# Two MLP products done with seven half-size block products in place of eight, their weight operands streamed from scratch memory

## The chip, the cores and the metric

The kernel runs on one core of a Trainium2 chip. The metric is the device time in microseconds (us) of one execution; a time quoted for a kernel is the median of its runs. All runs of one set ran on one chip, beside runs of the kernel before. A ratio is the mean time of one kernel's fast runs over the mean of the other's in the same rounds, so it is not quite the ratio of the two medians that stand beside it; 95% intervals are in square brackets.

Terms: TensorE does the matrix products; VectorE, ScalarE and GpSimd do the element-wise work. SBUF is the memory that the kernel keeps its operands in, PSUM the one that TensorE's results go to; a bank is in this text one buffer of a PSUM pool, and so one tile of the pool `ps_f`. The bank guard is a name for waits in the compiled program that the trace of the changed kernel shows: a product that goes to one half of a tile waits for the engine that reads the other half (192 waits, 115.8 us; in e_banks, with a tile for each sum, none). A pass is one matmul record of the trace; each fp32 matmul of the kernel leaves two (1152 records for the 576 matmuls of the up product before). The granted clock is the share of TensorE's full clock that the profile recorded.

## The reference, shortened to what matters

```python
# q, k, v: (8, 8, 576, 64) fp32; attention inside chunks of 64 tokens, then x: (8, 576, 512)
def _moe_ref(x, w_ch1, w_ch2):                 # w_ch1: 512 x 2048, w_ch2: 2048 x 512
    X = np.fft.fft(np.fft.fft(x, axis=1), axis=2)
    u = x + np.real(X).astype(np.float32)
    un = (u - mean(u)) / np.sqrt(var(u) + 1e-06)          # over the last axis
    ch = np.maximum(un @ w_ch1, 0.0) @ w_ch2              # the two MLP products
    return (u + ch).astype(np.float32)
```

The weights arrive in double precision; the kernel rounds them to fp32 itself.

## The kernel before

The 4608 token rows are worked through in nine groups of 512. In each group TensorE does the up product (16 outputs of 128 x 512, four matmuls each) and the down product (four outputs, 16 matmuls each). The attention and Fourier work of the next batch is slipped in between: `mlp` is a generator, and at each `yield` some of that side work is issued. From the eighth group on there is none left; I call the eighth and the ninth the quiet groups. Before the first group, and beside it, the weights are rounded.

```python
ps_t = ctx.enter_context(tc.tile_pool(name="ps_t", bufs=2, space=bass.MemoryType.PSUM))
ps_a = ctx.enter_context(tc.tile_pool(name="ps_a", bufs=2, space=bass.MemoryType.PSUM))
ps_f = ctx.enter_context(tc.tile_pool(name="ps_f", bufs=2, space=bass.MemoryType.PSUM))
...
def round_weight(i):                          # cut: one 128 x 512 piece of the weights
    ...
    nc.vector.tensor_scalar(wi, hi, 0x000FFFFF, None, ALU.bitwise_and)
    nc.vector.tensor_scalar(p, hi, 0x7FF00000, None, ALU.bitwise_and)
    # cut: three ScalarE steps; then for the piece before:
    nc.vector.scalar_tensor_tensor(w, lo, 2.0 ** -52, w, ALU.mult, ALU.add)
    nc.vector.scalar_tensor_tensor(p, hi, 0x80000000, p, ALU.bitwise_and, ALU.bitwise_or)
    nc.gpsimd.tensor_tensor(out=w, in0=w, in1=p.bitcast(FP32), op=ALU.mult)
...
def mlp(g):
    unT = unTs.pop(g)
    h1 = one_p.tile([128, KF, G * 128], FP32, tag="big", name="h1")
    for m in range(KF):                                        # up product, KF = 16
        up = ps_f.tile([128, G * 128], FP32, tag="ff", name="up")
        for kk in range(KD):                                   # KD = 4
            nc.tensor.matmul(out=up[:, 0:cols], lhsT=w1[:, kk, m * 128:(m + 1) * 128],
                             rhs=unT[:, kk, 0:cols], start=(kk == 0), stop=(kk == KD - 1))
        nc.scalar.activation(out=h1[:, m, 0:cols], in_=up[:, 0:cols], func=ACTF.Relu)
        yield
    for s, n in enumerate(groups[g]):                          # down product
        dn = ps_f.tile([128, 512], FP32, tag="ff", name="dn")
        for m in range(KF):
            nc.tensor.matmul(out=dn, lhsT=h1[:, m, s * 128:(s + 1) * 128], rhs=w2[:, m, :],
                             start=(m == 0), stop=(m == KF - 1))
            # cut: transposes of the next group, yields
        nc.vector.tensor_tensor(out=o, in0=dn, in1=natural(n), op=ALU.add)
        store(n, o)
        yield
```

Of the kernel before, what the change touches and what calls it, by code (L numbers as in the profile page):

```python
# [8 lines left out]
FP32 = mybir.dt.float32  # L9
# [7 lines left out]
def kernel(  # L17
# [52 lines left out]
    three_p = ctx.enter_context(tc.tile_pool(name="three", bufs=3))  # L70
    sm_p = ctx.enter_context(tc.tile_pool(name="sm", bufs=4))
    ps_t = ctx.enter_context(tc.tile_pool(name="ps_t", bufs=2, space=bass.MemoryType.PSUM))
    ps_a = ctx.enter_context(tc.tile_pool(name="ps_a", bufs=2, space=bass.MemoryType.PSUM))
    ps_f = ctx.enter_context(tc.tile_pool(name="ps_f", bufs=2, space=bass.MemoryType.PSUM))

    ident = const.tile([128, 128], FP32, name="ident")
    sign = const.tile([128, 1], FP32, name="sign")
# [4 lines left out]
    cd = const.tile([128, 2, HM + 1], FP32, name="cd")  # L82
    cs = const.tile([128, DM], FP32, name="cs")
    sd = const.tile([128, HM - 1], FP32, name="sd")
    w1 = const.tile([128, KD, DFF], FP32, name="w1")
    w2 = const.tile([128, KF, DM], FP32, name="w2")


    LO, HI, RE = "lo", "hi", "rest"
# [26 lines left out]
    def xt(n):  # L116
        return xall[:, place[n], 0:DM + 1]
# [16 lines left out]
    def load(n):  # L134
        for src, dst, nm, eng in ((q, qs, "q", nc.sync), (k, ks, "k", nc.scalar if n == 0 else nc.sync)):
            if n < first[1]:
                i = 2 * n + (nm == "k")
                t = start[:, (4 + i) * DM:(5 + i) * DM].rearrange("p (h d) -> p h d", h=H)
            else:
                t = two_p.tile([128, H, D], FP32, tag=nm, name=nm)  # L140
            (b0, c0), (b1, c1) = chunks(n)
            if b0 == b1 and c1 == c0 + 1:
                parts = [(0, 128, b0, c0)]
            else:
                parts = [(0, CH, b0, c0), (CH, CH, b1, c1)]
            for p0, np_, b, c in parts:
                eng.dma_start(  # L147
                    out=t[p0:p0 + np_], in_=src[b, :, c * CH:c * CH + np_, :].rearrange("h p d -> p h d")
                )
            dst[n] = t  # L150
# [98 lines left out]
    def att_T(n):  # L249

        a = qs.pop(n)
        pt = turn(lambda j: a[:, 2 * j:2 * j + 2, :].rearrange("p h d -> p (h d)"))
        t = one_p.tile([128, 2 * NJ, CH + 1], FP32, tag="qT", name="qT")
        low = kind(n) == LO
        nc.scalar.copy(t[:, :, CH:0:-1] if low else t[:, :, 0:CH], pt.rearrange("p j (c t) -> p (j c) t", c=2))  # L255
        if low:
            nc.gpsimd.tensor_copy(t[:, :, 0:1], t[:, :, CH:CH + 1])  # L257
        qT[n] = t
        a2 = ks.pop(n)
        pt = turn(lambda j: a2[:, 2 * j:2 * j + 2, :].rearrange("p h d -> p (h d)"))  # L260
        t = one_p.tile([128, NJ, 128], FP32, tag="kT", name="kT")
        nc.vector.tensor_copy(t, pt)  # L262
        kT[n] = t

    def att_S(n):
        a, b = qT.pop(n), kT.pop(n)
# [63 lines left out]
    def shift(b):  # L330

        lows = [xt(at[LO, b, i]) for i in range(NM)]
        r = b % 2 * CH
        rest = xt(rests[b // 2])[r:r + 1, 0:DM]
        t = three_p.tile([128, XW], FP32, tag="y", name="first")
        for i in range(NM):
            nc.sync.dma_start(out=t[2 * i:2 * i + 2, 0:DM], in_=lows[i][0:CH + 1:CH, 0:DM])
        nc.sync.dma_start(out=t[2 * NM:2 * NM + 1, 0:DM], in_=rest)
        for i in range(NM):
            nc.sync.dma_start(out=lows[i][0:CH + 1:CH, 0:DM], in_=t[2 * i + 1:2 * i + 3, 0:DM])  # L340
        nc.sync.dma_start(out=rest, in_=t[0:1, 0:DM])

    def fold(b, i):

# [27 lines left out]
    def attention(b):  # L372

        lo, hi = first[b], first[b + 1] - 1

        def ready(n):
            if n == at[LO, b, NM - 1]:
                shift(b)
            for i in range(NM):
                if n == at[HI, b, i]:  # L380
                    fold(b, i)
            if n == at[HI, b, 0]:
                fold(b, NM)

        if b == 0:
            att_T(0)
        for n in range(lo, hi + 1):
            att_S(n)
            yield
            if n + 1 < NT:  # L390
                att_T(n + 1)
                if n + 3 < NT and n + 3 >= first[1]:
                    load(n + 3)
            yield
            if n > lo:
                att_V(n - 1)
                if n + 2 < NT:
                    load_v(n + 2)
                ready(n - 1)
                yield  # L400
            att_P(n)
            yield
        att_V(hi)
        if hi + 3 < NT:
            load_v(hi + 3)
        ready(hi)
        yield
# [97 lines left out]
    def turned(g, s):  # L505
# [8 lines left out]
        else:  # L514
            nc.scalar.copy(unT[:, :, s * 128:(s + 1) * 128], pt)  # L515

    def store(n, o):

        if kind(n) == LO:
            b, c = chunks(n)[0]  # L520
            to = out[b, c * CH + 1:c * CH + 129, :].rearrange("(c p) d -> c p d", c=2)
            nc.sync.dma_start(out=to[:, ::-1], in_=o)
            return
        for h, (b, c) in enumerate(chunks(n)):
            r0, t0 = h * CH, c * CH
            if kind(n) == RE:
                nc.sync.dma_start(out=out[b, t0 + 1:t0 + CH, :], in_=o[r0 + 1:r0 + CH])
                nc.sync.dma_start(out=out[b, 0:1, :], in_=o[r0:r0 + 1])
            else:
                nc.sync.dma_start(out=out[b, t0:t0 + CH, :], in_=o[r0:r0 + CH])  # L530

    PARTS = 4
    N_MLP = KF + G * PARTS
    N_READY = KF + 2 * PARTS

    def mlp(g):

        unT = unTs.pop(g)
        cols = 128 * len(groups[g])
        h1 = one_p.tile([128, KF, G * 128], FP32, tag="big", name="h1")  # L540
        for m in range(KF):
            up = ps_f.tile([128, G * 128], FP32, tag="ff", name="up")
            for kk in range(KD):
                nc.tensor.matmul(  # L544
                    out=up[:, 0:cols],
                    lhsT=w1[:, kk, m * 128:(m + 1) * 128],
                    rhs=unT[:, kk, 0:cols],
                    start=(kk == 0),
                    stop=(kk == KD - 1),
                )  # L550
            nc.scalar.activation(out=h1[:, m, 0:cols], in_=up[:, 0:cols], func=ACTF.Relu)  # L551
            yield
        for s, n in enumerate(groups[g]):
            dn = ps_f.tile([128, 512], FP32, tag="ff", name="dn")
            for m in range(KF):
                nc.tensor.matmul(  # L556
                    out=dn,
                    lhsT=h1[:, m, s * 128:(s + 1) * 128],
                    rhs=w2[:, m, :],
                    start=(m == 0),  # L560
                    stop=(m == KF - 1),
                )
                if m % (KF // PARTS) == KF // PARTS - 1:
                    i = s * PARTS + m // (KF // PARTS)
                    if g + 1 < NG:
                        for j in range(G):
                            due = G * PARTS - (2 * (G - j) if g > 0 else G - j + 1)
                            if i == due - 1:
                                normed(g + 1, j)
                            if i == due:  # L570
                                turned(g + 1, j)
                    if m < KF - 1:
                        yield
            o = three_p.tile([128, DM], FP32, tag="o", name="o")
            nc.vector.tensor_tensor(out=o, in0=dn, in1=natural(n), op=ALU.add)  # L575
            store(n, o)
            yield

    with tc.manual_schedule():
        make_identity(nc, ident)  # L580
# [26 lines left out]
        def round_next():  # L607
            nonlocal n_w
            if n_w <= len(pieces):
                round_weight(n_w)  # L610
                n_w += 1
# [25 lines left out]
        for b in range(1, B):  # L637
            n_tiles = first[b + 1] - first[b]
            sizes.append(4 * n_tiles + 4 + NM + b % 2)
        done, cur = 0, 0  # L640
        t = 0
        for g in range(NG):
            for _ in mlp(g):
                t += 1
                round_next()
                if t % 2:
                    round_next()
                if cur < len(sides):
                    t0 = KF + 1 if cur == 0 else N_READY + (cur - 1) * N_MLP + (2 if cur == 1 else 0)
                    t1 = N_READY + cur * N_MLP + (2 if cur == 0 else 0)  # L650
                    due = min(sizes[cur], (t - t0) * sizes[cur] // (t1 - t0 - 1))
                    while done < due:
                        next(sides[cur], None)
                        done += 1
                    if t >= t1 - 1:
                        for _ in sides[cur]:
                            pass
                        cur, done = cur + 1, 0
# [49 lines left out]
```

## Time and profile before

| | before |
|---|---|
| time, median of its first 3 runs | 1326.65 us (1326.09 to 1328.92) |
| profiled span, granted TensorE clock | 1325.4 us, 0.987 |
| TensorE busy | 1278.1 us, 96% |
| moved by DMA | 57.01 MB, 43 GB/s |
| first product starts / second group starts | 87.23 / 258.47 us |
| groups 2 to 7, mean of one | 140.0 us |
| eighth group | 111.6 us |

How to read it: the starts come from the TensorE timeline (the first row of the up product's line in each group), and a group's time is the difference of two of them; groups 2 to 7 are (1098.37 - 258.47) / 6. The first row of the second group, before:

```profile
258.47 3.60 PE L544 MATMUL up<-unT,w 128*128 128x512 f32 x8
```

A group is 110 us of MLP and, up to the seventh, some 30 us of attention and Fourier work on the same engine.

### The profile page before, as it was taken

What the parts mean: (1) busy time and instruction counts of PE and PEld (TensorE: products, weight loads), DVE (VectorE), ACT (ScalarE), POOL (GpSimd) and SP (SyncE); (2) the same over time, 40 slices, a digit from 0 to 9 for tenths busy, and PEclk for the clock granted to TensorE, in tenths of its full rate; (3) what the DMA queues carried; (4) which work ended last, traced back from release to release, by engine and by line L of the source; (5) the groups of instructions that cost most, each with busy time, mean ns of one, the idle gap of its engine ahead of it and who ended that gap; (6) DMA issues with size and microseconds to landing.
All of it is one profiled execution on the core that took longest, in us unless ns stands there. A gap on an engine that the chain in (4) does not pass through costs nothing.

```text
span 1325.4 us, 13849 instructions
## 1 busy us (share of the span) xinstructions
PE 1278.1 (96%) x5708; PEld 624.4 (47%) x5708; DVE 347.9 (26%) x648; ACT 253.6 (19%) x517; POOL 129.9 (10%) x188
## 2 busy tenths in 40 slices
PE   7788889999999999999999999999999999999998
PEld 5453344544444445444544445444444444444443
DVE  4479942421231114220321033211311130000000
ACT  3257620121011201121112111210111001100100
POOL 0135411002000201002100110020002010000000
PEclk9899988999999999999999999999999999999999
DMA  8634530221012101211022002210100000000000
GB/s 197 157 96 150 158 79 19 51 45 40 10 37 52 32 8 30 59 32 29 21 48 47 10 17 56 43 39 8 33 17 0 9 17 8 0 16 16 0 8 24
DMA packets 126261, 57.01 MB, mean 43 GB/s; under 512 B 116533, under 2 KB 117046, under 8 KB 126198
## 3 DMA queue, kind: packets, MB, share of 16 engines
q1 hardware_dynamic: 124598, 55.73, 17.1%
q8 instruction: 45, 0.74, 0.2%
q10 hardware_dynamic: 1600, 0.39, 0.2%
q14 instruction: 18, 0.15, 0.0%
HBM read 46.50 MB, written 9.44 MB: 42 GB/s over the span
## 4 chain that ended last, share of the span: by engine, by line
PE 85%; DVE 5%; DMA 3%; issue 2%; SPq 2%; ACT 1%; POOL 1%; POOLq 0%; DVEq 0%
PE dn L556 36%; PE up L544 34%; PE pt L245 4%; PE z L421 4%; PE mix L464 3%; DVE power L226 1%; PE xp L310 1%; DMA xall<-in_moe_w_ch_dram 1%; PE sc L272 1%; DVE power L234 1%; DVE w L224 1%; PE z L431 1%; SPq L157 1%; DVE w L233 1%; SPq L147 1%
## 5 line engine op out<-in xcount | busy, mean ns | idle before, releaser
L544 PE MATMUL up<-unT,w 128*128 128x512 f32 x1152 | 515.5, 598 | 8.6 <-ACT h L551 7.7
L556 PE MATMUL dn<-w,h 128*128 128x512 f32 x1152 | 518.5, 599 | 0.0
L544 PEld LDWEIGHTS up<-unT,w 128*128 128x128 f32 x1152 | 212.7, 190 | 253.7 <-issue 237.1
L556 PEld LDWEIGHTS dn<-w,h 128*128 128x128 f32 x1152 | 214.0, 191 | 246.6 <-issue 244.7
L551 ACT ACTIVATE h<-up 128x512 f32<-128x512 f32 x144 | 85.7, 595 | 423.9 <-PE up L544 423.8
L575 DVE TENSOR_TENSOR o<-dn,xall 128x512 f32<-128x512 f32 x36 | 24.8, 690 | 250.4 <-PE dn L556 250.4
L281 DVE TENSOR_REDUCE mx<-sc 128x8 f32<-128x512 f32 x36 | 24.9, 691 | 208.0 <-PE sc L272 208.0
L319 DVE TENSOR_TENSOR xall<-xp,rd 128x512 f32<-128x512 f32 x36 | 24.9, 690 | 131.2 <-PE xp L310 131.2
L479 POOL TENSOR_TENSOR xall<-y,xall 128x513 f32<-128x513 f32 x16 | 27.6, 1724 | 262.8 <-DVE y L472 262.8
L235 POOL TENSOR_TENSOR w<-w,power 128x512 f32<-128x512 f32 x32 | 44.6, 1395 | 65.9 <-DVE power L234 65.9
L421 PE MATMUL z<-tk,pm 128*128 128x289 f32 x128 | 37.9, 417 | 4.0 <-POOL pm L365 4.0
L439 ACT COPY zf<-z 128x256 f32<-128x256 f32 x32 | 11.9, 371 | 151.2 <-PE z L421 109.4
L289 ACT ACTIVATE ex<-ex 128x512 f32<-128x512 f32 x36 | 22.7, 629 | 94.1 <-DVE ex L283 94.1
L262 DVE COPY kT<-pt 128x512 f32<-128x512 f32 x36 | 24.5, 681 | 51.8 <-PE pt L245 51.8
L310 PEld LDWEIGHTS xp<-v,pT 64*64 64x64 f32 x1152 | 20.8, 138 | 30.0 <-issue 21.8
L421 PEld LDWEIGHTS z<-tk,pm 128*128 128x128 f32 x128 | 23.9, 192 | 22.1 <-issue 13.7
L257 POOL COPY qT<-qT 128x8 f32<-128x8 f32 x16 | 3.2, 201 | 314.1 <-ACT qT L255 314.1
L272 PEld LDWEIGHTS sc<-kT,qT 64*64 64x64 f32 x1152 | 21.3, 141 | 23.4 <-issue 23.4
L515 ACT COPY unT<-pt 128x512 f32<-128x512 f32 x18 | 10.5, 585 | 111.6 <-PE pt L245 111.6
L310 PE MATMUL xp<-v,pT 64*64 64x64 f32 x1152 | 25.8, 229 | 5.8 <-ACT pT L300 5.8
L291 DVE TENSOR_REDUCE rd<-ex 128x8 f32<-128x512 f32 x36 | 24.7, 686 | 25.0 <-ACT ex L289 25.0
L605 PE MATMUL idle<-warm 128*128 128x289 f32 x92 | 30.2, 466 | 0.0
(90 smaller groups left out, 791.8 us busy)
## 6 DMA issues: line engine op xcount, KB each, us to landing
xall<-in_moe_w_ch_dram SPq DMA_DIRECT2D x32, 512.0 KB
v<-in_v_dram SPq DMA_DIRECT2D x142, 64.0 KB
q<-in_q_dram SPq DMA_DIRECT2D x34, 128.0 KB
k<-in_k_dram SPq DMA_DIRECT2D x34, 128.0 KB
out_dram<-o SPq DMA_DIRECT2D x16, 256.0 KB
out_dram<-o SPq DMA_DIRECT2D x32, 128.0 KB
q<-in_q_dram SPq DMA_DIRECT2D x14, 256.0 KB
k<-in_k_dram SPq DMA_DIRECT2D x14, 256.0 KB
```

What stands on the lines that cost most here:

```text
L235: nc.gpsimd.tensor_tensor(out=w, in0=w, in1=p.bitcast(FP32), op=ALU.mult)
L245: nc.tensor.transpose(pt[:, j, :], src(j), ident)
L272: nc.tensor.matmul(out=sc[t0:t0 + CH, e, j * CH:(j + 1) * CH], lhsT=a[r0:r0 + D, 2 * j + c, 0:CH], rhs=b[r0:r0 + D, j, t0:t0 + CH], start= ...
L281: nc.vector.tensor_reduce(out=mx, in_=s4, axis=AX.X, op=ALU.max)
L310: nc.tensor.matmul(out=xp[t0:t0 + CH, e, j * D:(j + 1) * D], lhsT=a[r0:r0 + CH, j, t0:t0 + CH], rhs=b[r0:r0 + CH, c, j, :], start=True, st ...
L421: nc.tensor.matmul(out=z[:, 0:NQ], lhsT=pm[p, fold_, half], rhs=tk[p, i, fold_, :], start=(i == 0), stop=(i == NM), skip_group_check=(T == 2),
L464: nc.tensor.matmul(out=o[:, cols], lhsT=zt[:, T], rhs=tab, start=(T == 0), stop=(T == 3), skip_group_check=True,)
L479: eng.tensor_tensor(out=x[:, 0:w], in0=y[:, 0:w], in1=x[:, 0:w], op=ALU.add)
L544: nc.tensor.matmul(out=up[:, 0:cols], lhsT=w1[:, kk, m * 128:(m + 1) * 128], rhs=unT[:, kk, 0:cols], start=(kk == 0), stop=(kk == KD - 1),)
L551: nc.scalar.activation(out=h1[:, m, 0:cols], in_=up[:, 0:cols], func=ACTF.Relu)
L556: nc.tensor.matmul(out=dn, lhsT=h1[:, m, s * 128:(s + 1) * 128], rhs=w2[:, m, :], start=(m == 0), stop=(m == KF - 1),)
L605: nc.tensor.matmul(out=idle[:, 0:NQ], lhsT=warm[:, 0:128], rhs=warm[:, 0:NQ], start=True, stop=True)
```

## The change

Its intent: write each product as a 2 x 2 product of blocks and do it with seven products of half-size blocks for eight, as in the Strassen-Winograd scheme. TensorE then does 448 passes of 256 columns per group for 256 of 512 columns, an eighth less work. The price: the seven weight operands (some are sums of blocks) take 7/4 of the weights' room and are not kept on chip; they are formed once, beside the first group, stored to scratch memory, and streamed back in slabs by each later group; and the partial results are put together by VectorE, ScalarE and GpSimd. The first group still does eight products. The core of the diff:

```diff
-    ps_a = ctx.enter_context(tc.tile_pool(name="ps_a", bufs=2, space=bass.MemoryType.PSUM))
-    ps_f = ctx.enter_context(tc.tile_pool(name="ps_f", bufs=2, space=bass.MemoryType.PSUM))
+    ps_a = ctx.enter_context(tc.tile_pool(name="ps_a", bufs=1, space=bass.MemoryType.PSUM))
+    ps_f = ctx.enter_context(tc.tile_pool(name="ps_f", bufs=4, space=bass.MemoryType.PSUM))
+    dram = ctx.enter_context(tc.tile_pool(name="dram", bufs=1, space=bass.MemoryType.DRAM))
...
-                t = two_p.tile([128, H, D], FP32, tag=nm, name=nm)
+                t = one_p.tile([128, H, D], FP32, tag=nm, name=nm)
...
+    def keep1(f, kk):                    # four GpSimd sums and seven stores; keep2 is like it
+        ...
+            nc.gpsimd.tensor_tensor(out=out_, in0=in0, in1=in1, op=op)
+        to = s1.rearrange("m p (o k f) -> p m o k f", o=NO, k=2)
+        for o, a in enumerate((a11, o2, o1, o3, a12, o4, a22)):
+            nc.sync.dma_start(out=to[:, 4 * f:4 * f + 4, o, kk], in_=a.rearrange("p (m f) -> p m f", m=4))
...
+    def fetch(which):
+        i = n_slab[which]
+        if i < N_SLAB[which]:
+            ...
+            nc.sync.dma_start(out=dst, in_=src[i % n])
...
+        for m in range(HF):              # up product, 8 steps
+            w = slab1[i % NS]
+            pa = ps_f.tile([128, 2, 256], FP32, tag="ff", name="pa")
+            pb = ps_f.tile([128, 2, 256], FP32, tag="ff", name="pb")
...
+            product(0, unT[:, 0:2, lo], pa[:, 0], True)
+            nc.scalar.copy(a, pa[:, 0])
+            product(1, tt[:, 1], pa[:, 1], False)
+            nc.vector.tensor_tensor(out=b, in0=pa[:, 1], in1=a, op=ALU.add)
+            product(2, tt[:, 0], pb[:, 0], True)
+            nc.vector.tensor_tensor(out=a, in0=pb[:, 0], in1=b, op=ALU.add)
+            product(3, unT[:, 0:2, hi], pb[:, 1], False)
+            nc.vector.tensor_tensor(out=h1[:, HF + m, hi], in0=pb[:, 1], in1=a, op=ALU.add)
+            if m > 0:
+                operands(m - 1)
+            yield
+            product(4, unT[:, 2:4, lo], pa[:, 0], False)
+            nc.scalar.activation(out=h1[:, m, lo], in_=pa[:, 0], func=ACTF.Relu)
+            product(5, unT[:, 2:4, hi], pb[:, 0], False)
+            nc.vector.tensor_tensor(out=h1[:, m, hi], in0=pb[:, 0], in1=b, op=ALU.add)
+            nc.scalar.activation(out=h1[:, m, hi], in_=h1[:, m, hi], func=ACTF.Relu)
+            product(6, tt[:, 2], pb[:, 1], False)
+            nc.vector.tensor_tensor(out=h1[:, HF + m, lo], in0=pb[:, 1], in1=b, op=ALU.add)
...
+                if g == 0 and conv and n_w > (KD * KF // 4 if len(conv) > HF // 2 else len(pieces)):
+                    conv.pop(0)()        # keep1 and keep2, beside the first group
```

Cut: the down product (its two halves alternate over two pairs of banks), the attention schedule, the final sums. In the text "product 1" is `product(0, ...)`, and so on to product 7.

## The prediction

> **What bounds the kernel now.** I read the page first (busy shares, slices, chain), then the TensorE timeline of the quiet end, then the same timeline of the first group, and last the groups by shape for the durations of half-size work.
>
> ```profile
> PE 1278.1 (96%) x5708; PEld 624.4 (47%) x5708; DVE 347.9 (26%) x648; ACT 253.6 (19%) x517; POOL 129.9 (10%) x188
> PE   7788889999999999999999999999999999999998
> PE dn L556 36%; PE up L544 34%; PE pt L245 4%; PE z L421 4%; PE mix L464 3%; DVE power L226 1%; PE xp L310 1%; DMA xall<-in_moe_w_ch_dram 1%; PE sc L272 1%; DVE power L234 1%; DVE w L224 1%; PE z L431 1%; SPq L157 1%; DVE w L233 1%; SPq L147 1%
> ```
>
> TensorE is the bound: 96% busy, full from slice 7 on, and 70% of the chain that ended last is the two MLP products. In the last groups nothing else is left:
>
> ```profile
> 1209.99 55.10 PE L544 MATMUL up<-unT,w 128*128 128x512 f32 x128
> 1264.92 55.10 PE L556 MATMUL dn<-w,h 128*128 128x512 f32 x128
> ```
>
> The first product starts at 1209.99 and the second at 1264.92, so 128 passes take 54.93 us, 429 ns each, without a gap. A group costs 256 passes, 109.9 us; nine groups 989 of the 1326 us. So removing passes from TensorE removes time, if nothing makes TensorE wait.
>
> The first group is different. Its products wait for the rounding of the weights on VectorE, ScalarE and GpSimd:
>
> ```profile
> 112.93 7.13 PE L544 MATMUL up<-unT,w 128*128 128x512 f32 x16 [1.42 <-ACT h L551]
> 121.81 7.13 PE L544 MATMUL up<-unT,w 128*128 128x512 f32 x16 [1.75 <-ACT h L551]
> ...
> 121.04 1.39 POOL L235 TENSOR_TENSOR w<-w,power 128x512 f32<-128x512 f32 x1 [1.56 <-DVE power L234]
> 121.22 1.49 DVE L226 TENSOR_SCALAR power<-xall 128x512 uint32<-128x512 uint32 x1
> 149.99 0.41 DVE L226 TENSOR_SCALAR power<-xall 128x512 uint32<-128x512 uint32 x1
> ```
>
> Sixteen passes every 8.88 us instead of 6.87. The same VectorE instruction takes 0.41 us alone and 1.49 us beside a GpSimd operation: the two hold each other up. This stage has no slack on VectorE and GpSimd, which matters below. The first product starts at 87.2 us and the second group at 258.5.
>
> [...]
>
> **The change, part by part.**
>
> *Passes removed.* Per group the up product becomes 8 steps of 7 products of 2 matmuls, the down product 7 of 8 matmuls for two halves: 224 matmuls of 256 columns, 448 passes. Their price from the existing half-size passes:
>
> ```profile
> 226.13 1.03 PE L464 MATMUL mix<-cd,zf 128*128 128x257 f32 x4
> 227.00 1.02 PE L464 MATMUL mix<-cs,zf 128*128 128x512 f32 x2
> 227.86 0.59 PE L464 MATMUL mix<-sd,zf 128*128 128x255 f32 x2
> 228.29 4.03 PE L556 MATMUL dn<-w,h 128*128 128x512 f32 x9
> ```
>
> Start to start: four of 257 in 0.87 us (217 ns), two of 255 in 0.43 (215). I take 215.5 ns: 448 passes are 96.5 us against 109.9, 13.3 us saved per group, 107 us over eight groups. The transposes, attention and Fourier passes stay.
>
> *Waits added in the up product.* I read the compiled program's semaphores for one of the 8 steps. Products 1 and 2 share a PSUM bank (pa), 3 and 4 another (pb), then 5 goes to pa, 6 and 7 to pb. Because of the bank guard product 2 waits for ScalarE's copy of product 1, product 4 for VectorE's sum from product 3, product 7 for VectorE's sum from product 6. (Products 3 and 5 wait for nothing new; 6 waits for a sum that product 5 covers.) The attention work is inserted after product 4 and after product 7, never into these three holes. The size of one hole, from four rows:
>
> ```profile
> L439 ACT COPY zf<-z 128x256 f32<-128x256 f32 x32 | 11.9, 371 | 151.2 <-PE z L421 109.4
> ...
> L472 DVE TENSOR_TENSOR y<-y,mix 128x255 f32<-128x255 f32 x20 | 8.4, 420 | 0.7
> ...
> 85.14 1.22 PE L245 MATMUL pt<-ident,un 128*128 128x128 f32 x8
> 87.23 1.10 PE L544 MATMUL up<-unT,w 128*128 128x512 f32 x2 [0.88 <-DVE unT L513]
> ```
>
> There TensorE ends at 86.36, VectorE's 0.69 us copy lies between, TensorE restarts 0.88 us later: 0.19 us for the two handovers. A half-size pass lasts about 0.38 us where the next could start after 0.215, so 0.17 us of pipeline is no longer overlapped. [...] A ScalarE hole is 0.17 + 0.19 + 0.37[...] = 0.84 us, a VectorE hole 0.89. Per step 0.84 + 2 x 0.89 = 2.6 us on 28 x 0.2155 = 6.0; per group 8 x 2.6 = 21 us, 167 us over eight groups. It is more than the saving: the up product should go from 55 to about 69 us, the down product, whose two halves alternate so that each sum has 3.4 us to finish, from 55 to 48.
>
> *More on the path behind these waits.* The VectorE chain of an attention score (max, subtract, wait for ScalarE's exponential, sum, reciprocal: 3.3 us at 166.5 to 169.7) can now stand ahead of a sum that TensorE waits for. Two to three scores fall into an up product, an estimated 1.2 to 2.3 us each: 3 us per group in the six groups that still have attention beside them, 18 us. And each step has a GpSimd subtraction beside a VectorE one[...]; by the blocking seen at 121.22 I give 2 us per group, 16 us.
>
> *First group.* Sixteen GpSimd operations (1.4 us, L235) form the combined weights while rounding still runs, sixteen more after it; each set of four waits for the stores of the set before it. In the order of the changed program two of the later sets stand ahead of GpSimd's small copy that the first attention score needs, and TensorE stands behind that score. First half: 4 x (5.6 + 2.1) = 31 us of GpSimd work where VectorE had 18, less two rounds of buffer, about 12 us. Second half: 2 x 6 to 7 us, about 13. The single q/k buffer, with loads queued behind the stores, about 5. The prologue loses a 3.8 us wait for a q load: -3. [...] Sum about +29 us, the least certain term.
>
> *Streaming.* A slab is 0.92 or 1.05 MB, one per about 8 us: some 125 GB/s besides the 33 GB/s of now. At the start the kernel moves 197 GB/s at 80% busy and 158 at 50%, and three slabs give two steps of lead. I count it as hidden. VectorE rises by about 9 instructions of 0.42 us per step, far from full.
>
> Sum: 1326.65 - 107 + 167 + 18 + 16 + 29 = 1449.65. I shade this to 1440, since some GpSimd blocking may fall into holes already counted.
>
> **Rivals.** (1) *TensorE stays dense:* if the holes close (restart overlapped, sums done early), the time is 1326.65 - 107 + 29, about 1250. For it: the full TensorE row and four PSUM banks for this work. Against it: each hole is inside one bank, so more banks do not help, and existing restarts show 0.19 us plus the whole operation. (2) *Holes half as long:* about 1326.65 - 107 + 84 + 29 + 10, some 1343, a tie. [...] (3) *The stream binds:* if slabs arrive at less than 110 GB/s or behind small loads in the one queue, a step grows to 9 to 10 us; 1480 to 1550. Against it: GB/s seen at the start. (4) *VectorE binds* in the up product: about 2.9 us new per 8.6 us step, plus 30 us per group of attention now; no.
>
> **Range and chances.** The saving and the holes rest on durations in the trace; 15% on the holes is 25 us, the first group is uncertain by 15, the blocking by 15: together some 35 to 45 us. 1390 to 1485. A gain over 2% needs holes below half a microsecond: 5%. Within 2%: 7%. Slower by over 2%: 88%.
>
> **What would show it.** Right: in the last group without attention, up about 69 us and down about 48; TensorE idle before the up product's line 110 us or more, released by ScalarE's copy and VectorE's sums in about 192 waits of 0.5 to 0.7 us; passes at 215 ns start to start in the down product; the second group starting near 288 us. Wrong: an up product near 48 us (the holes close), up waits released by DMA (the stream), passes above 230 ns, or a second group at 260.

The trace before shows this: a matmul of 128 x 512 is two passes, 429 ns each; the passes of 257 columns, each with its own weight load, start 217 ns apart; VectorE's additions last 690 ns at 512 elements and 420 at 255, 61%. That a product waits for the reader of its bank was the author's reading of the compiled program's waits.

A term is cut from the sum of a hole, which came to 0.84 us behind ScalarE and 0.89 behind VectorE: the three terms that stand make 0.73 and 0.78. From the first group's sum of +29 a term for the first slab is cut; the terms that stand, 12 + 13 + 5 - 3, make 27. The total of 1449.65, shaded to 1440, stands with both in it. The 0.38 us of a half-size pass is the row at 227.86 (two passes in 0.59, less 0.215).

In the first group, 2.1 us agrees with one and a half pieces of the rounding at 1.4 us (L235), and 18 with four times one and a half pieces at 2.96 us (the spacing of VectorE's rounding, 118.27 to 121.22); the 5 for the q/k buffer was an estimate without a measured source. That VectorE and GpSimd hold each other up is in the trace before in both directions: beside the 1.49 us stands one GpSimd instruction of L235 that took 3.28 us for its usual 1.39 (at 103.14, with four VectorE instructions beside it that lost nothing). Where the operands lie is not shown to matter.

## The result, and the profile after

The changed kernel took 1426.81 us (1423.01 to 1430.39, 4 runs) beside 1326.83 us (1326.09 to 1328.92, 4 runs) of the kernel before: ratio 1.075 [1.0714, 1.0786], slower. The record holds no check of this run's result; the same program but for one small copy (e_copy) was found correct. The profiled span is 1422.4 us at a granted clock of 0.974. From the page of the kernel after, busy times, TensorE's row of slices (the span in 40 parts, busy tenths) and what was moved:

```profile
PE 1223.7 (86%) x7244; PEld 901.1 (63%) x7244; DVE 587.0 (41%) x1224; ACT 296.3 (21%) x661; POOL 308.6 (22%) x370
...
PE   7797348987998889988997899879988998899898
...
DMA packets 164028, 189.43 MB, mean 133 GB/s; under 512 B 119461, under 2 KB 137382, under 8 KB 156774
```

TensorE lost work (1278.1 to 1223.7 us) and the span still grew: its share fell from 96% to 86%. The row shows it in two places, a deep dent in slices 4 to 6 (the first group) and eights all the way to the end, where the kernel before had nines.

The eights are the up product. From the TensorE timeline of the last group, where no attention stands beside it (start, duration, what, and in brackets the idle time before it and what ended that):

```profile
1301.66 1.03 PE L674 MATMUL pa<-unT,wa 128*128 128x256 f32 x4
1303.20 1.13 PE L674 MATMUL pa<-wa 128*128 128x256 f32 x4 [0.52 <-ACT wa L680]
1304.17 1.03 PE L674 MATMUL pb<-wa 128*128 128x256 f32 x4
1305.71 1.13 PE L674 MATMUL pb<-unT,wa 128*128 128x256 f32 x4 [0.52 <-DVE wa L684]
1306.68 1.03 PE L674 MATMUL pa<-unT,wa 128*128 128x256 f32 x4
1307.55 1.03 PE L674 MATMUL pb<-unT,wa 128*128 128x256 f32 x4
1309.09 1.13 PE L674 MATMUL pb<-wa 128*128 128x256 f32 x4 [0.52 <-DVE h L693]
1310.06 1.03 PE L674 MATMUL pa<-unT,wa 128*128 128x256 f32 x4
```

One row is one product. Products 5 and 6 (1306.68, 1307.55) start 0.87 us apart, as dense work does. Products 2, 4 and 7, each the second in a row on its bank, start 1.54 us after the one before: TensorE waits for ScalarE's copy or VectorE's sum, and after the wait the product takes 0.97 us to the next instead of 0.87. A hole behind VectorE therefore costs 0.68 + 0.10 = 0.78 us, and so does the first one behind ScalarE. From the second step on, ScalarE's copy stands behind a ReLU of 0.63 us, product 2 starts 1.60 us after product 1, and the hole costs 0.84 us. The whole up product runs from 1301.66 to 1369.23, 8.45 us a step, where seven dense products would be 6.04 us.

The down product keeps its promise; its rows, of 32 passes each, start 6.91 us apart, 216 ns a pass:

```profile
1369.23 7.07 PE L727 MATMUL pa<-wb,h 128*128 128x256 f32 x32
1376.14 7.07 PE L727 MATMUL pa<-wb,yall 128*128 128x256 f32 x32
```

The view of waits, TensorE alone, adds up the whole run (total us, times, longest):

```profile
PE pa L674 <- ACT wa L680: 42.6, 64, 1.4
PE pb L674 <- DVE h L693: 40.1, 64, 2.2
PE pb L674 <- DVE wa L684: 33.1, 64, 0.5
```

They are the waits of the bank guard: 192 waits, three in each of 64 steps, and 115.8 us; in e_banks, with a tile for each sum, none. In groups 2 to 7 fifteen of them are longer than the rest: ten behind ScalarE's copy (1.40 us, where it stands behind the exponential of an attention score, L310) and five behind VectorE's sum L693 (1.73 to 2.20 us, where it stands behind the last steps of a score, L314).

The dent in the first group, from the TensorE timeline there:

```profile
130.83 9.03 PE L613 MATMUL up<-unT,wa 128*128 128x512 f32 x16 [5.01 <-ACT h L620]
...
150.69 5.90 PE L613 MATMUL up<-unT,wa 128*128 128x512 f32 x8 [10.83 <-ACT h L620]
...
193.03 1.14 PE L293 MATMUL sc<-kT,qT 64*64 64x64 f32 x32 [27.62 <-POOL qT L276]
```

The longest waits of this stretch before were 2.15 us for ScalarE's ReLU and 3.99 us for GpSimd. The granted clock fell as well: it is 0.89 over the first group's up product and 0.84 over its down product, where before it was 0.97 and 0.92, and the eight passes at 150.69 take 5.90 us, where eight such passes in the last group before, at a clock of 1.00, take 3.4 (8 x 429 ns). VectorE's timeline shows one thing that holds up the up product there: the same rounding instruction lasts 0.42 us before GpSimd forms combined weights (its first such sum starts at 116.12) and 1.48 us while it does:

```profile
114.60 0.42 DVE L243 TENSOR_SCALAR wb<-xall 128x512 uint32<-128x512 uint32 x1
...
119.72 1.48 DVE L243 TENSOR_SCALAR wb<-xall 128x512 uint32<-128x512 uint32 x1
```

Where the time went, by the starts of the groups in the two TensorE timelines (the second group after the change starts with this row):

```profile
298.80 1.13 PE L674 MATMUL pa<-unT,wa 128*128 128x256 f32 x4
```

| | before | after | difference |
|---|---|---|---|
| second group starts | 258.47 | 298.80 | +40.3 |
| groups 2 to 7, mean of one | 140.0 | 147.5 | +7.5 each, +45.3 |
| eighth group | 111.6 | 117.7 | +6.1 |
| start of the ninth to the end of the span | 115.4 | 120.7 | +5.3 |

The sum is the 97 us by which the span grew. The first product starts 6.3 us earlier than before (80.95 for 87.23), so the first group itself grew by 46.6 us.

### The profile page after: what moved, and what is told of

It is laid out like the page before. It is cut to its first block, busy times and chain, and to the rows that moved or that the text cites. A ratio compares the mean times of both kernels' runs of the same rounds, so it can differ in the third digit from the quotient of the medians.

```text
span 1422.4 us, 18460 instructions
## 1 busy us (share of the span) xinstructions
PE 1223.7 (86%) x7244; PEld 901.1 (63%) x7244; DVE 587.0 (41%) x1224; ACT 296.3 (21%) x661; POOL 308.6 (22%) x370
## 4 chain that ended last, share of the span: by engine, by line
PE 73%; DVE 13%; ACT 5%; issue 3%; DMA 3%; POOL 3%; SPq 1%; POOLq 0%; ACTq 0%; DVEq 0%
PE pb L674 18%; PE pb L727 16%; PE pa L727 12%; PE pa L674 11%; PE pt L264 4%; PE z L441 3%; PE mix L484 3%; DVE wa L684 2%; DVE h L693 2%; PE dn L625 2%; DVE power L245 2%; DMA xall<-in_moe_w_ch_dram 2%; ACT wa L680 1%; PE xp L331 1%; PE sc L293 1%
## 5 line engine op out<-in xcount | busy, mean ns | idle before, releaser
L674 PE MATMUL pb<-wa 128*128 128x256 f32 x512 | 138.1, 392 | 40.1 <-DVE h L693 40.1
L674 PE MATMUL pb<-unT,wa 128*128 128x256 f32 x512 | 138.1, 392 | 33.1 <-DVE wa L684 33.1
L674 PEld LDWEIGHTS pb<-wa 128*128 128x128 f32 x512 | 92.0, 189 | 75.7 <-DVE h L693 65.8
L674 PE MATMUL pa<-unT,wa 128*128 128x256 f32 x512 | 136.6, 389 | 0.0
L674 PEld LDWEIGHTS pb<-unT,wa 128*128 128x128 f32 x512 | 91.9, 189 | 68.8 <-DVE wa L684 58.8
L727 PE MATMUL pa<-wb,h 128*128 128x256 f32 x512 | 115.6, 381 | 0.0
L727 PE MATMUL pb<-wb,h 128*128 128x256 f32 x512 | 115.1, 381 | 0.0
L674 PE MATMUL pa<-wa 128*128 128x256 f32 x256 | 72.4, 405 | 42.6 <-ACT wa L680 42.6
L727 PEld LDWEIGHTS pa<-wb,h 128*128 128x128 f32 x512 | 95.8, 190 | 16.2 <-issue 3.8
L727 PEld LDWEIGHTS pb<-wb,h 128*128 128x128 f32 x512 | 95.6, 190 | 12.7
L674 PEld LDWEIGHTS pa<-unT,wa 128*128 128x128 f32 x512 | 90.7, 190 | 16.4 <-issue 5.0
```

What stands on the lines that cost most here:

```text
L674: nc.tensor.matmul(out=out_, lhsT=w[:, o, kk], rhs=rhs[:, kk], start=(start and kk == 0), stop=(kk == 1), skip_group_check=True,)
L727: nc.tensor.matmul(out=dst, lhsT=lhs[:, m], rhs=w[:, m], start=(start and m == 0), stop=(m == HF - 1), skip_group_check=True,)
```

## The experiments

Theory: each of the three holes in a step comes from two products in a row on one PSUM bank with a reader between them; the rest of the loss is the forming of the combined weights beside the rounding in the first group. Rivals: the holes come from the chain of sums itself, the stream of weights sets the pace, the smaller buffers cost the time, or a small GpSimd copy in the first group does. Ten kernels were run, in three sets. The kernel before ran beside each set at 1327.12, 1326.68 and 1326.24 us; ratios are against those runs.

### e_banks: each partial sum in a bank of its own

The pool has four banks already; the change puts two half-bank sums in each tile and uses two tiles a step. This kernel uses four tiles a step, no more PSUM in all.

```diff
-            pa = ps_f.tile([128, 2, 256], FP32, tag="ff", name="pa")
-            pb = ps_f.tile([128, 2, 256], FP32, tag="ff", name="pb")
+            pw, px, py, pz = (
+                ps_f.tile([128, 2, 256], FP32, tag="ff", name=n_)[:, 0] for n_ in ("pw", "px", "py", "pz")
+            )
-            product(1, tt[:, 1], pa[:, 1], False)
+            product(1, tt[:, 1], px, True)
... (cut: products 1 and 5 go to pw, 3 and 6 to py, 4 and 7 to pz)
```

> The changed kernel (1426.8 us), with each of the up product's four partial sums in a PSUM bank of its own instead of two to a bank; the same products, sums, passes and bytes. Theory (the bank guard's three holes per step are the loss): the waits of products 2, 4 and 7 vanish, a step falls from 8.46 us to 6.1 to 6.5, 64 steps save 125 to 154 us: 1270 to 1300 us, faster than the kernel before. Rival A (the stream binds): slabs of 0.92 MB cannot arrive every 6 us; TensorE then waits for DMA at the head of a step, step 7.5 us or more, 1360 or more. Rival B (VectorE's chain of sums sets the pace): steps above 7 us with waits on VectorE. Result correct.

Measured: 1258.82 us (1258.55 to 1260.44), ratio 0.949 [0.9476, 0.9504], correct; 168 us below the change and below my range as well. The timeline of its last group has no brackets left, and the starts are 0.86 to 0.87 us apart:

```profile
1155.33 1.03 PE L675 MATMUL pw<-unT,wa 128*128 128x256 f32 x4
1156.20 1.03 PE L675 MATMUL px<-wa 128*128 128x256 f32 x4
1157.06 1.03 PE L675 MATMUL py<-wa 128*128 128x256 f32 x4
```

Its up product lasts 48.35 us (1155.33 to 1203.68), against 67.57. Of the 168 us, 8 x 19.2 = 154 are the holes as sized above; groups 2 to 7 lost 128.7 us in all (885.2 to 756.5), 13 more than six times 19.2. Those 13 are the longer waits behind attention scores: the idle time of groups 2 to 7 above the quiet pace is 13 us as well, and in this kernel no up product after the first group waits for a sum or a copy at all. So the holes come from the shared banks: with the same products, sums and passes none is left.

### e_one: product 2 alone in a third bank

```diff
+            pc = ps_f.tile([128, 2, 256], FP32, tag="ff", name="pc")
-            product(1, tt[:, 1], pa[:, 1], False)
-            nc.vector.tensor_tensor(out=b, in0=pa[:, 1], in1=a, op=ALU.add)
+            product(1, tt[:, 1], pc[:, 0], True)
+            nc.vector.tensor_tensor(out=b, in0=pc[:, 0], in1=a, op=ALU.add)
```

> The change, with product 2 alone taken out of product 1's bank (a third bank in a step); products 3 and 4 and 6 and 7 still share theirs. My theory (each hole stands by itself, and the one behind ScalarE's copy costs 0.84 us in each of 64 steps): 54 us less than the change, 1367 to 1379, the other two holes as long as before. Rival (the chain copy, sum, sum, sum sets the pace, and the other two waits grow by what this one loses): 1415 to 1427.

Measured: 1377.13 us (1372.19 to 1377.38), ratio 1.0376 [1.0357, 1.0396], 49.7 us less than the change. Its TensorE waits in the up product:

```profile
PE pb L675 <- DVE wa L685: 42.2, 64, 1.4
PE pb L675 <- DVE h L694: 40.1, 64, 2.2
```

The wait for ScalarE is gone, product 7's is the same to the tenth, product 4's grew by 9 us: ten of its waits are 1.41 us now, each where the sum of product 2 stands late behind ScalarE's copy, so the delay by the exponentials moved to it. In the last group the up product is 60.96 us, so 6.6 us or 0.83 a step went away. The holes stand by themselves and add up, with that small remainder; the rival, in which the other waits take over all of the 42.6 us, is rejected.

### e_three: three banks, no two products in a row on one

Products 1 and 5 are on one bank, 3 and 6 on another, 2, 4 and 7 on the third.

```diff
+            pc = ps_f.tile([128, 2, 256], FP32, tag="ff", name="pc")
-            product(1, tt[:, 1], pa[:, 1], False)
+            product(1, tt[:, 1], pc[:, 0], True)
-            product(3, unT[:, 0:2, hi], pb[:, 1], False)
+            product(3, unT[:, 0:2, hi], pc[:, 1], False)
-            product(6, tt[:, 2], pb[:, 1], False)
+            product(6, tt[:, 2], pc[:, 1], False)
```

> Three banks in a step: products 1 and 5, 3 and 6, 2, 4 and 7, so that no two products in a row touch one bank, though banks are still shared. My theory (what costs is only that the guard's reader stands between two products in a row; one product of 0.86 us is long enough for a sum of 0.42): as fast as a bank for each, 1255 to 1263. Rival (a shared bank costs at any distance, as product 4 must wait for the sum of 2): 10 us or more slower than 1258.8.

Measured: 1271.02 us (1270.31 to 1271.23), ratio 0.9586 [0.957, 0.9602]. That is a miss: 12 us above e_banks (the two ran in different sets, the ratios 0.9586 and 0.949 say the same), where I had put them equal. In the quiet groups it is as dense as e_banks: the last up product takes 48.35 us too. The difference lies in groups 2 to 7, 768.7 us against 756.5. The TensorE timeline of the third group, and VectorE's at the same time:

```profile
454.08 1.03 PE L675 MATMUL pb<-wa 128*128 128x256 f32 x4
455.99 1.13 PE L675 MATMUL pc<-unT,wa 128*128 128x256 f32 x4 [0.88 <-DVE wa L683]
```

```profile
454.50 0.69 DVE L312 TENSOR_REDUCE rd<-ex 128x8 f32<-128x512 f32 x1 [0.69 <-ACT ex L310]
455.22 0.17 DVE L313 TENSOR_SCALAR rd<-rd 128x8 f32<-128x8 f32 x1
455.43 0.20 DVE L314 RECIPROCAL rd<-rd 128x8 f32<-128x8 f32 x1
455.55 0.39 DVE L683 TENSOR_TENSOR wa<-pc,wa 128x256 f32<-128x256 f32 x1
```

Product 4 waits for the sum of product 2 (L683), and that stands behind the last steps of an attention score. Ten such waits are in the trace, 8.8 us of idle; with the restarts each costs 1.05 us here (454.08 + 0.86 = 454.94 to 455.99). So a shared bank with one product between cost nothing while the reader was prompt (48.35 us, as with a bank each), and cost a wait of up to 0.9 us where the reader's engine did something else first. In e_banks product 4's bank was last used by product 7 of the step before, three products earlier, and none of these waits is left.

### e_nostream and e_banks_nostream: without the stream

The loads of the weight slabs after the first three are left out, on the change and on e_banks. The results are wrong (relative error 0.349).

```diff
-            nc.sync.dma_start(out=dst, in_=src[i % n])
+            if i < NS:
+                nc.sync.dma_start(out=dst, in_=src[i % n])
```

> The changed kernel without any slab load after the first three of each kind: the products run on stale slabs, so the result is wrong on purpose; every other instruction stays. Theory: the stream is hidden, the time stays within 4 us of 1426.8. Rival A (the stream costs time already): 15 us or more faster.

> Own banks, without the loads of the weight operands after the first three (wrong result on purpose). The stream is hidden also behind TensorE without holes: within 4 us of own banks alone, 1255 to 1262. Rival (with the holes gone the stream begins to set the pace): 10 us or more faster than 1258.8.

Measured: 1424.89 us (1421.93 to 1429.8) for the first, ratio 1.0752 [1.0728, 1.0775], and 1258.35 us (1255.89 to 1259.99) for the second, ratio 0.9482 [0.9467, 0.9496]. Both are their kernels' times. The table by stretches for groups 2 to 7 (length, then busy time of PE, PEld, DVE, ACT, POOL with counts, clock, DMA share, GB/s), first of the change, then without its stream:

```profile
298.80:1184.00 885.20, 794.57 (x5043) 612.57 (x5038) 353.24 (x791) 163.28 (x399) 166.08 (x222) 1.00 0.42 130
```

```profile
298.80:1184.00 885.20, 794.48 (x5038) 612.45 (x5037) 352.88 (x790) 163.29 (x399) 166.06 (x222) 1.00 0.14 32
```

DMA fell from 130 to 32 GB/s and the stretch stayed the same. The stream is hidden, also behind a TensorE without holes, where it runs at 153 GB/s in that stretch.

### e_bufs: only the changed buffers

All nine groups do eight whole products; what remains of the change is its SBUF and PSUM layout, the single q and k buffers, and the attention schedule that goes with them.

```diff
+    NF = NG
-        conv += [lambda i=i: keep2(i) for i in range(HF // 2)]
+        conv = []
-            for _ in (mlp(g) if g else mlp_first(g)):
+            for _ in (mlp(g) if g >= NF else mlp_first(g)):
... (cut here and in the next runs with NF: the counters and the attention schedule that follow from it)
```

> Only the changed SBUF buffers of the change; eight whole products for every up and down product, no combined weights, no scratch memory. My theory (the buffers cost nothing once the groups run; the loss is in the bank guards and in the first group's conversion): within 6 us of the kernel before, 1321 to 1333. Rival (the smaller buffers themselves cost the later groups 6 us each): 1365 to 1380.

Measured: 1318.5 us (1316.35 to 1319.42), ratio 0.9934 [0.992, 0.9949]. The rival falls; and it is 8 us faster than the kernel before, 2.5 below my range. The second group starts at 255.72 for 258.47, and groups 2 to 7 take 139.2 for 140.0 us each. Which of the moved buffers and loads gives this was not taken apart.

### e_conv: those buffers and the combined weights, eight products throughout

As e_bufs, but the combined weights are formed and stored beside the first group, as in the change, and then not used.

```diff
+    NF = NG
-            for _ in (mlp(g) if g else mlp_first(g)):
+            for _ in (mlp(g) if g >= NF else mlp_first(g)):
-                    for _ in range(NS):
-                        fetch(1)
```

> The changed kernel's buffers and its making and storing of the combined weights in the first group, but all nine groups by the eight whole products and no slab ever loaded. Theory: the first group's extra (second group starting 40.3 us later) is all that remains over the kernel before: 1327 + 36 to 42, so 1363 to 1369 us. If the single attention bank or the single q/k buffer also cost in the later groups: more than 1372. If the 40 us were partly the wait for the first slab: less than 1360. Result correct.

Measured: 1361.11 us (1358.81 to 1361.67), ratio 1.0255 [1.024, 1.0271], 43 us above e_bufs and 2 us below my range, a small miss: the layout alone is faster than the kernel before, which I had not counted. Second group at 297.60, which is 41.9 later; from there on the two are alike (139.2 us each for groups 2 to 7). So forming the weights costs 42 us, all in the first group: 20.6 in its up product (76.7 us against 56.1) and nearly all the rest after it. Part of it is the clock: TensorE does the same passes in the first group in 158.5 busy us for 151.3, and the granted clock over the whole span is 0.971 for 0.987 in e_bufs; the other 34 us are idle time.

### e_copy: GpSimd's small copy on ScalarE

The first attention score waits 27.62 us for a copy of 128 x 8 elements that stands behind the combined weights in GpSimd's order. This kernel gives the copy to ScalarE.

```diff
-            nc.gpsimd.tensor_copy(t[:, :, 0:1], t[:, :, CH:CH + 1])
+            nc.scalar.copy(t[:, :, 0:1], t[:, :, CH:CH + 1])
```

> The changed kernel with the small copy of one column of q (128x8) on ScalarE instead of GpSimd, so that the first attention score of the first group no longer stands behind GpSimd's combined weights (a wait of 27.6 us in the trace). Simple theory: about 25 us faster. My theory: the next transposition needs a q load that the DMA queue issues only after the stores of two sets of combined weights (issued at 193.7 us, landed at 198.6), so the wait moves to that load and the gain is 0 to 4 us. Result correct.

Measured: 1425.89 us (1424.4 to 1426.23), ratio 1.0745 [1.0729, 1.0761]: no gain. The same stretch of its TensorE timeline:

```profile
182.62 1.14 PE L293 MATMUL sc<-kT,qT 64*64 64x64 f32 x32 [15.88 <-DVE kT L281]
...
199.74 1.08 PE L264 MATMUL pt<-ident,q 128*128 128x128 f32 x4 [15.98 <-DMA q<-in_q_dram]
```

The wait only changed its name: now it is VectorE's copy behind the rounding, then a q load. The longest wait of a view is not yet a cause.

### e_late: combined weights beside the second group

Conversion in the second group, which then also does eight products; seven products from the third group on; banks as in the change.

```diff
+    NF = 2
-                if g == 0 and conv and n_w > (KD * KF // 4 if len(conv) > HF // 2 else len(pieces)):
+                if g == NF - 1 and conv and (t - begin[g]) % 3 == 1:
-                if t == begin[1] - 1:
+                if t == begin[NF] - 1:
```

> The change, with the conversion of the weights moved from the first group to the second, so seven products from the third group on; banks as in the change. My theory (some 38 us were lost in the first group because its up and down products read the same whole weights and small loads that the conversion holds up; and a seven-product group with shared banks costs some 6 to 7 us more than an eight-product one): if the conversion is beside as much work in the second group it costs less there, as weights lie ready: 1378 to 1400. Rival (the conversion costs the same wherever it stands, by its own length on VectorE and GpSimd): 1415 to 1425.

Measured: 1379.17 us (1378.28 to 1380.66), ratio 1.0397 [1.0379, 1.0414], 47.6 below the change. The second group starts at 255.94, as in e_bufs (255.72), and lasts 141.8 us against 140.5 there. Forming the weights costs 1.3 us beside the second group and 42 beside the first; the same 32 operations on GpSimd and the same stores. They are not spread wider: they take from 256.6 to 341.4 us here and from 117.7 to 214.6 in e_conv. The rest of the gain, 47.6 - 40.6 = 7 us, is close to what one group fewer with the holes is worth (147.5 us against 139.2 in e_bufs). Two later groups are 2.0 and 1.7 us longer than in the change; why is not shown.

### e_banks_late: both

The edits of e_banks and of e_late together:

```diff
+    NF = 2
-            pa = ps_f.tile([128, 2, 256], FP32, tag="ff", name="pa")
-            pb = ps_f.tile([128, 2, 256], FP32, tag="ff", name="pb")
+            pw, px, py, pz = (
...
+                if g == NF - 1 and conv and (t - begin[g]) % 3 == 1:
... (cut: the rest of the two edits)
```

> Own bank for each of the four partial sums, and the conversion in the second group. My theory: from the 1258.8 us of own banks alone, minus the 30 to 38 us of the first group, plus some 15 us for one group more with eight products: 1232 to 1248, the fastest version. Rival (conversion costs the same wherever it stands): 1270 to 1278, slower than own banks alone.

Measured: 1229.52 us (1227.56 to 1231.02), ratio 0.9265 [0.9251, 0.9279], correct. It is the fastest version, 7% below the kernel before and 2 to 3 us below my range: 40.6 us less in the first two groups and 13.2 more for a whole group of eight products make 27.4, and e_banks minus this is 29.3. TensorE is busy 96% again.

## Why the prediction was right

It said slower, 1440 us, 1390 to 1485; the change took 1426.81. Its main mechanism, TensorE made to wait three times a step by shared banks, is shown by its cause removed: the kernel without the shared banks is 168 us faster. The terms of its sum against what the runs showed:

| term | predicted | measured | from |
|---|---|---|---|
| passes removed | -107 | -105 | last group of e_banks 96.7 us against 109.9, times eight |
| holes in the up product | +167 | +154 | last up product 67.57 against 48.35 (e_banks), times eight |
| attention scores ahead of sums | +18 | +13 | groups 2 to 7, e_banks against the change, less the holes |
| GpSimd beside VectorE | +16 | none seen | the sums last 0.37 to 0.43 us in all steps of the change |
| first group | +29 | +40 | start of the second group |
| buffers in the later groups | none | -4 | e_bufs, groups 2 to 7 |
| sum | +123, shaded to +113 | +98 | times: 1426.81 - 1326.83 = +100 |

*Passes and down product:* 215.5 ns a pass was predicted, 216 measured; the down product 48 us, measured 48.3. Each pass has its own weight load (7244 records of each in the trace after), and two of 256 columns take 432 ns for 429 of one of 512, so halving the products cost next to nothing there.

*Holes:* up product 69 us predicted, 67.6 measured; 192 waits foretold, 192 found, 0.52 us each in most steps of the quiet groups (0.57 behind ScalarE's copy). A VectorE hole is 0.78 us for the predicted 0.89. ScalarE's 0.84 was met by luck: it is 0.78 where the copy starts at once, and 0.84 only because a ReLU that was not in the working delays the copy. The terms that still stand, 0.17 us for the end of the pass before, 0.19 for the handovers and 0.42 for VectorE's sum, make 0.78 by themselves. In the trace the 0.78 is made up otherwise: 0.52 of idle, 0.16 by which a pass's record lasts longer (0.38) than the start of the next is away in dense work (0.216), and 0.10 after the restart. What the 0.10 consists of is not shown.

*Attention:* the effect is real, the size was 13 for 18, and the path was half of it: five of the fifteen long waits are behind VectorE's part of a score, as predicted; ten are behind ScalarE's exponential, which the prediction had only as something VectorE waits for. (That chain lasts 3.2 us by the two times given, not 3.3.)

*GpSimd beside VectorE in the groups:* this step failed. I took the blocking seen in the rounding (0.41 us alone, 1.49 beside GpSimd) for every group; that every pair of the two behaves so was my estimate. The pair that I had in mind, in the last group of the change:

```profile
1324.58 0.42 DVE L662 TENSOR_TENSOR yall<-wb,h 128x256 f32<-128x256 f32 x1
1324.69 0.90 POOL L663 TENSOR_TENSOR h<-h 128x256 f32<-128x256 f32 x1 [7.56 <-DVE wb L661]
```

In all 64 steps VectorE's instruction starts 0.04 to 0.14 us before GpSimd's and lasts 0.42 to 0.43 us, as the sums do that have nothing beside them. So VectorE lost nothing, and there was nothing for TensorE to wait for. (The prediction's "about 9" VectorE instructions a step are 7 in the program; its 2.9 us fit the 7.)

*First group:* undersized. Conversion costs 42 us for a predicted 25 (12 + 13), about 8 more in each half. The layout's own part came out near its terms: the first product starts 5.7 us earlier in e_bufs (3 predicted) and the first group is 3.0 us longer (5 predicted), together -2.7 for +2. The errors, 11 too little here and 13, 5, 16 and 4 too much in holes, attention, GpSimd and buffers, partly cancel, and the shading by 10 took off some more; that the total is so near is in part luck.

*Rivals:* "TensorE stays dense", put at about 1250, is what e_banks does at 1258.82. My reason against it, "each hole is inside one bank, so more banks do not help", may hold for more tiles of two sums each (not run), and is wrong as a limit of the kernel: one sum per tile, from the same four banks, closes every hole. The stream as the bound is refuted by both runs without it.

Two things stay open: why the changed layout alone is 8 us faster, and how the 42 us in the first group divide between VectorE held up by GpSimd, the weight loads queued behind stores, the order of GpSimd's work, and the lower clock in the same stretch (some 7 us by the busy times above). That they vanish when the same work is moved one group later shows only that it is the meeting with what the first group has of its own, the rounding and the loads above all.

## What to carry to other kernels

The change packed two half-bank results into a tile, so that a product had to wait for the reader of the one before it: a product of 0.86 us that followed another on its bank lost 0.78 us behind a VectorE sum of 0.42 us, and 0.84 behind a ScalarE copy of 0.35 us that was itself late. Three such places a step ate one and a half times what an eighth less work saved; with a bank for each sum (e_banks) these losses were gone. So when a change makes results smaller, count banks and not bytes: no two products in a row on a bank that someone reads between, and more distance where the reader's engine also does other work. One product in between was enough in the quiet groups (48.35 us, as with a bank each) and cost 12 us in all where attention delayed the reader (e_three). One-time work is best tried where its engines are idle and nothing waits: the same conversion cost 42 us in the first group and 1.3 in the second.
